# Two blocks' last residual added by VectorE from PSUM, the 14th down chunk on 128 rows, and a new written order

## The chip, the cores and the metric

The kernel runs on one core of a Trainium2 chip. A core has TensorE (PE, matmuls, with a separate row PEld for the loading of the stationary operand), VectorE (DVE), ScalarE (ACT), GpSimd (POOL) and SyncE (SP, which here issues most transfers). Matmuls write PSUM, the other engines work between PSUM and SBUF. The metric is the device time of one launch in microseconds, as the median of three runs.

## The reference

The layer is a convolution block (A) with a gated feed-forward block (B) behind it, both with a residual. There are 2048 tokens of width 640; the hidden width of B is 1728. Inputs are bf16. Cut to what matters:

```python
def _A_ref(q, k, v, shift_k, ssm_k, ssm_D):
    k_shift = sum(k_pad[:, t:t + S, :] * shift_k[:, ks - 1 - t] for t in range(4))
    kv = k_shift * v
    y = irfft(rfft(kv, 2 * S) * rfft(ssm_k, 2 * S))[:S]        # causal convolution, per channel
    return q * (y + kv * ssm_D)

def _B_ref(x, w_gate, w_up, w_down):
    return (silu(x @ w_gate) * (x @ w_up)) @ w_down

x = A_q
h = x + _A_ref(_layernorm(x), A_k, A_v, A_shift_k, A_ssm_k, A_ssm_D)
return h + _B_ref(_layernorm(h), B_w_gate, B_w_up, B_w_down)
```

The hidden width 1728 is 13 chunks of 128 and one of 64. The 64-wide chunk is the "14th chunk" of the title.

## The kernel before, in words

**Blocks.** The tokens are cut into four blocks of 512 (0 to 3). A token tile is the 128 tokens of a block with the same remainder by 4, so a block has four of them, called positions 0 to 3. The convolution is done as block-wise transforms: matmuls against cosine and sine tables (`halves` and `quads`, matmul lines 581 and 619), products of spectra on VectorE (`prod`, line 783), and the inverse transform by matmuls (`inverse`, lines 939 and 944). The short filter over four tokens is done by many small matmuls that use the array in row groups of 32 or 64 rows (`taps`, line 732).

**Work of one block i.** Its x, k and v are loaded (`x2`, `kT2`, `v2` are the loads of block 2, and so on), `tp` and `xf` are the taps and the forward transform, `p` the products, `yb` the butterflies ahead of the inverse, `iv` the inverse. Behind each `iv` tile stands a chain of small steps: `ive` (ScalarE out of PSUM), `ivg` (VectorE, gate with x), `ivm` and `ivs` (ScalarE, mean and square), `ivv` (VectorE), `ivr` (GpSimd, power), `ivn` (normalised row) and `ht` (a transposing DMA into `hnT`). `hnT` is the moving operand of the feed-forward matmuls. `kt`, `kf`, `kb`, `kc` prepare the spectra of the filter in blocks of their own.

**Feed-forward (`ffn`).** Gate and up products are made in two halves of 256 tokens (positions 0, 1 and 2, 3). For each half there are four groups of chunks; `fg` and `fu` are the matmul groups (line 1049, 20 matmuls of 256 columns, 15 in the last group), `sg` is silu on ScalarE into `gu`, `su` a scaled copy of the up part into `ub`, `mu` the product on VectorE. There is one buffer `ub`, so each `su` waits for the `mu` before it. The fourth group holds chunk 12 and the 64-wide chunk 13; its gate and up columns are packed in one stationary tile `PK` (64 gate rows above 64 up rows), so `sv` copies the up part of chunk 13 from PSUM rows 64 to 127.

**Down projection.** `dn` accumulates 14 chunks into two PSUM halves of 320 columns (line 1135; line 1012 for the last token tile, which is split in two). For chunk 13 the rows are shared out: `gd` copies rows 0 to 63 of `gu[:, 13]` to rows 64 to 127 (lines 1111 and 1112), the weight's columns 0 to 319 lie on rows 0 to 63 and its columns 320 to 639 on rows 64 to 127, and the two 64-row matmuls use different row groups of the array (`PAIR`). Odd positions begin with chunk 13 and even ones end with it.

**Last residual.** For blocks 0, 1 and 2 (`RD`), `rs` moves the down result and the mean from PSUM to a buffer `RB` (line 1151 on ScalarE, line 1152 on VectorE), and `ra` adds `RB` onto x by an accumulating DMA from the GpSimd queue (`addto`, line 568). There is one `RB`. For block 3 a VectorE instruction adds PSUM, mean and x in one step (line 1156; line 1018 for the split tile). `out` stores the tile from the SP queue.

**PSUM.** The eight banks are used as four units of two banks. Each matmul group opens one unit (`tp` with 32-row groups opens two) and must wait until the group that had the unit before has been read out.

**Order.** `PLAN` holds, for each engine, the written order of all its steps, and the unit of each PSUM tile. An engine runs its list strictly in that order, with waits where a step depends on another engine. 

Of the kernel before, what the change touches and what calls it, by code (L numbers as in the profile page):

```python
# [50 lines left out]
class _Graph:  # L51
# [131 lines left out]
    def emit(self, block):  # L183
# [84 lines left out]
    "act":  # L268
# [9 lines left out]
    "dve":  # L278
# [15 lines left out]
        "806 ",  # L294
    "units":
        "0113201022031012033321231021332312133313321010001232312221313201230311022320230103301222001112012120120312322323013103"
        "23101021312302023330210213103130021301200122003201320321302",
# [948 lines left out]
```

## Time and profile before

| what | value |
|---|---|
| median of three runs | 254.49 us (254.41 to 254.68) |
| profiled execution, its own time | 254.13 us |
| span of the program in that execution | 252.2 us |
| busy PE / DVE / ACT / POOL | 243.4 / 195.5 / 184.7 / 58.7 us |
| granted TensorE clock | 1.0 |

A row of the timeline has the start and the length in microseconds, the engine, the line, the operation, the tiles written and read, and in brackets the idle time before it with the step that ended it. A row of the chain of waits has a start, a length and what filled it. A matmul's length in the profile contains its latency; matmuls overlap, so the pace of a row of matmuls is its length divided by their count.

### The profile page before, as it was taken

To read this page: it belongs to the slowest core of one execution; us is meant where nothing else is said; L and a number is where in the kernel's file an instruction comes from. 1 tells how busy PE (TensorE), PEld (TensorE's weight loads), DVE (VectorE), ACT (ScalarE), POOL (GpSimd) and SP (SyncE) were. 2 spreads that over 40 slices of the span, in tenths; PEclk is the share of its full clock that TensorE was granted. 3 is DMA by queue.
4 is the path that set the end of the run, shared out by engine and by line. 5 is a ranking of instruction groups with operands and counts; after the bars stand their busy time and mean duration, and the time that the engine had idled before them with its cause. 6 is when DMAs were issued, how large, how long until landed. Compare 5 with 4: busy or idle time off the path is not lost.

```text
span 252.2 us, 5601 instructions
## 1 busy us (share of the span) xinstructions
PE 243.4 (96%) x2405; PEld 190.7 (76%) x2405; DVE 195.5 (78%) x249; ACT 184.7 (73%) x303; POOL 58.7 (23%) x62
## 2 busy tenths in 40 slices
PE   7998997999999999999999999999999999999995
PEld 3776574688887867888888765888886678888763
DVE  2899999999989999999999896989959321312322
ACT  2499999999897994678999699478982856543500
POOL 1000033443113457602103333211141122100000
PEclk9999999999999999999999999999999999999999
DMA  6999999989994465999914718795871144300003
GB/s 212 338 316 222 389 381 292 142 154 169 274 176 78 141 104 109 174 169 216 208 19 76 189 26 82 169 232 99 146 140 26 23 85 79 81 0 3 0 29 104
DMA packets 39063, 37.04 MB, mean 147 GB/s; under 512 B 21235, under 2 KB 34046, under 8 KB 39038
## 3 DMA queue, kind: packets, MB, share of 16 engines
q1 hardware_dynamic: 31648, 23.56, 35.0%
q0 software_dynamic: 7376, 13.11, 30.7%
q8 instruction: 19, 0.31, 0.5%
q14 instruction: 6, 0.05, 0.0%
q10 hardware_dynamic: 14, 0.01, 0.0%
HBM read 16.29 MB, written 2.62 MB: 75 GB/s over the span
## 4 chain that ended last, share of the span: by engine, by line
PE 73%; DVE 11%; DMA 8%; ACT 5%; issue 1%; SPq 0%; DVEq 0%
PE ps L1049 45%; PE ps L1135 18%; PE ps L581 4%; DMA kvo<-in_A_v_dram 3%; DVE C L561 2%; PE ps L944 2%; DVE tt L783 2%; DMA hnT<-qo 2%; PE ps L1012 2%; DMA k0n<-in_A_k_dram 2%; PE ps L732 1%; DVE kvo L755 1%; DVE Y L783 1%; DMA xh<-RB 1%; DVE kvo L748 1%
## 5 line engine op out<-in xcount | busy, mean ns | idle before, releaser
L1135 PE MATMUL ps<-Wd,gu 128*128 128x320 bf16 (+1 forms) x420 | 58.4, 300 | 0.3 <-ACT qo L954 0.3
L1135 PEld LDWEIGHTS ps<-Wd,gu 128*128 128x128 bf16 (+1 forms) x420 | 38.9, 97 | 18.7 <-issue 2.8
L783 DVE TENSOR_TENSOR tt<-XH,C 128x2560 bf16<-128x2560 bf16 (+1 forms) x29 | 45.1, 1576 | 0.2
L1070 DVE TENSOR_TENSOR gu<-gu,ub 128x1024 bf16<-128x1024 bf16 (+1 forms) x32 | 19.9, 621 | 20.9 <-ACT gu L1057 12.9
L1057 ACT ACTIVATE gu<-ps 128x1024 bf16<-128x1024 f32 (+1 forms) x32 | 29.0, 913 | 8.7 <-PE ps L1049 8.5
L1049 PE MATMUL ps<-hnT,GB 128*128 128x256 bf16 x280 | 34.2, 273 | 0.0
L1049 PE MATMUL ps<-hnT,UB 128*128 128x256 bf16 x280 | 33.7, 273 | 0.0
L1062 ACT ACTIVATE ub<-ps 128x1024 bf16<-128x1024 f32 x24 | 24.5, 1020 | 12.4 <-PE ps L1049 9.7
L1049 PEld LDWEIGHTS ps<-hnT,UB 128*128 128x128 bf16 x280 | 27.4, 98 | 3.3
L1049 PEld LDWEIGHTS ps<-hnT,GB 128*128 128x128 bf16 x280 | 27.2, 98 | 3.3
L1049 PE MATMUL ps<-hnT,UA 128*128 128x256 bf16 x240 | 28.8, 273 | 0.0
L1049 PE MATMUL ps<-hnT,GA 128*128 128x256 bf16 x240 | 28.2, 273 | 0.4 <-DMA hnT<-qo 0.4
L1049 PEld LDWEIGHTS ps<-hnT,GA 128*128 128x128 bf16 x240 | 23.4, 98 | 3.5 <-DVE OS L458 0.8
L1049 PEld LDWEIGHTS ps<-hnT,UA 128*128 128x128 bf16 x240 | 23.3, 98 | 3.1 <-ACT XH L455 0.2
L857 POOL TENSOR_TENSOR mv<-mv,half 128x1 f32<-128x1 f32 x16 | 15.7, 982 | 32.9 <-DVE mv L855 28.5
L581 PE MATMUL ps<-KT,tab 128*128 128x320 bf16 x128 | 19.4, 300 | 2.3 <-DVE KT L457 1.1
L860 ACT ACTIVATE qo<-xh 128x640 bf16<-128x640 bf16 x28 | 20.6, 736 | 1.2 <-DMA hnT<-qo 0.5
L954 ACT ACTIVATE qo<-ps,one,st 128x640 bf16<-128x640 f32 x16 | 13.8, 883 | 8.1 <-PE ps L939 7.1
L568 POOL DMA_DIRECT2D xh<-RB x12 | 10.8, 899 | 38.0 <-ACT RB L1151 31.6
L581 PEld LDWEIGHTS ps<-KT,tab 128*128 128x128 bf16 x128 | 11.3, 98 | 8.8 <-DVE KT L457 1.4
L857 POOL TENSOR_TENSOR st<-st,half 128x4 f32<-128x4 f32 x4 | 7.2, 1792 | 38.7 <-DVE st L852 31.4
L862 ACT ACTIVATE qo<-xh,mv 128x640 bf16<-128x640 bf16 x16 | 13.2, 830 | 0.2
(115 smaller groups left out, 377.0 us busy)
## 6 DMA issues: line engine op xcount, KB each, us to landing
C<-US POOLq DMA_DIRECT2D x6, 640.0 KB, 6.6
kc<-in_A_ssm_k_dram SPq DMA_DIRECT2D x4, 640.0 KB, 9.9
xh<-in_A_q_dram SPq DMA_DIRECT2D x4, 640.0 KB, 6.9
out_dram<-xh SPq DMA_DIRECT2D x15, 160.0 KB, 1.9
kvo<-in_A_v_dram SPq DMA_DIRECT2D x3, 640.0 KB, 7.6
xh<-RB POOLq DMA_DIRECT2D x12, 160.0 KB, 2.9
C<-C POOLq DMA_DIRECT2D x2, 640.0 KB, 7.6
Wd<-in_B_w_down_dram SPq DMA_DIRECT2D x1, 1280.0 KB, 11.8
```

Of the source, the lines that this page charges most:

```text
L568: return g.add(name, "pool", lambda e, n: e.dma_start(dst, src, accum_op=ALU.add, max_dma_last_dim=4096), ("acc", 2 * int(np.prod(dst.shap ...
L581: last = e.matmul(pt.f(c, W), tab[:, f, cs, j], src[:, j, c * W:(c + 1) * W], start=(j == js[0]), stop=(j == js[1]))
L783: g.add(nm, "dve", lambda e, n_: e.tensor_tensor(out=d, in0=a, in1=b, op=op), ("sb", n * D), r=[a, b], w=[d])
L857: g.add(name + "r", "pool", lambda e, n: e.tensor_tensor(out=dst, in0=tmp, in1=hf, op=ALU.pow), ("pp", 4), r=[tmp, half[:]], w=[dst])
L860: g.add(name + "m", "act", lambda e, n: e.activation(out=junk, in_=x, func=ACTF.Identity, scale=-1.0 / D, accum_out=sm), ("aa", D, 0), r=[ ...
L862: g.add(name + "s", "act", lambda e, n: e.activation(out=junk, in_=x, func=ACTF.Square, bias=sm, accum_out=sq), ("aa", D, 1), r=[x, sm], w ...
L954: g.add(nm + "e", "act", lambda e, n, pt=pt, q2=q2, s=s, j=j: e.activation(out=q2, in_=pt.f2(W), func=ACTF.Identity, scale=s[:, 3, j:j + 1 ...
L1049: last = e.matmul(pt.f(q // 2, 256, o=256 * (q % 2)), w[:, c, f0:f0 + P], hnT[:, c, cols], start=(c == 0), stop=(c == NC5 - 1))
L1057: g.add("sg%d.%d%d" % (i, h, gp), "act", lambda e, n, pa=pa, gv=gv, nf=nf: e.activation(out=gv, in_=pa.f(0, 256 * nf).rearrange("p (f x) - ...
L1062: g.add("su%d.%d%d" % (i, h, gp), "act", lambda e, n, pb=pb: e.activation(out=ub[:].rearrange("p b x -> p (b x)"), in_=pb.f(0, 1024), func ...
L1070: g.add("mu%d.%d%d" % (i, h, gp), "dve", lambda e, n, gv=gv, ubv=ubv: e.tensor_tensor(out=gv, in0=gv, in1=ubv, op=ALU.mult), ("sb", 256 * ...
L1135: last = e.matmul(pt.f(c, W), gu[k, fb, col(i, j)], Wd[k, fb, c * W:(c + 1) * W], start=st, stop=sp)
```

## The change

`RD` goes from (0, 1, 2) to (0,): in blocks 1 and 2, `rs` becomes the VectorE instruction of line 1156 and the eight `ra` transfers are gone. `PAIR` goes from True to False: chunk 13 of the down projection is two 128-row matmuls like the other chunks, rows 64 to 127 of its weight are set to zero once (`wz`, a memset), both column halves of the weight come by one load, the eight `gd` copies are gone, and `mu` of the fourth group is cut into two products of 256 columns (`mu` on 128 rows, `mv` on 64). Chunk 13 always comes last in `dn`. All five orders and the PSUM units are new.

The orders of the diff hold step numbers; these are counted again in the new kernel, since some steps are gone and some new. By name, these are the moves of steps between engines: `k0e2` ACT to DVE, `kf0e.011` DVE to ACT, `xf0e.110` ACT to DVE, `kte2.1` DVE to ACT, `kf2e.110` and `kf3e.011` ACT to DVE, `ke2.4` ACT to DVE, `la1.3x`, `la3.1x` ACT to DVE, `la2.3x`, `la3.3x` DVE to ACT, `xf3e.10`, `xf3e.20` DVE to ACT, `xf3e.01` ACT to DVE, `lp0`, `lp2`, `la2w` DVE to POOL, `la3w` POOL to DVE. In the SP queue `x1` moves from behind `UA` to just behind `kT1`, `itab` from ahead of `GA` to behind it, `WdC` from ahead of `itab` to behind `ht0.0`, and `WdA` from behind `ht0.2` to ahead of it.

```diff
-    RD = (0,1,2)
+    RD = (0,)
-    PAIR = True
+    PAIR = False
...
+        if not PAIR:
+            g.add("wz", "pool dve", lambda e, n: e.memset(Wd[:, 13, :], 0.0), ("pm", D), w=[Wd[:, 13, :]])
...
+                    if nf == 2 and not PAIR:
+                        for nm, a, b in (("mu", gu[:, 12, cols], u12), ("mv", gu[0:FL, 13, cols], u13)):
+                            g.add("%s%d.%d%d" % (nm, i, h, gp), "dve", lambda e, n, a=a, b=b: e.tensor_tensor(out=a, in0=a, in1=b, op=ALU.mult),
+                                  ("sb", 256), r=[a, b], w=[a])
+                        continue
...
-                if col(i, j).start // P % 2:
+                if PAIR and col(i, j).start // P % 2:
                     seq = [13] + seq[:-1]
...
-                                k = slice(0, P) if fb < 13 else slice(FL * c, FL * c + FL)
+                                k = slice(0, P) if fb < 13 or not PAIR else slice(FL * c, FL * c + FL)
```

By name, the new order of the PE list in the stages that the prediction speaks of:

```
block 1:       dn0.3 fu1.00 tp2.0 tp2.4 fg1.00 fu1.01 xf2.30 xf2.11 xf2.10 xf2.31 fg1.01 xf2.01 xf2.20 fg1.02 ...
into block 2:  dn1.1 iv2.1 iv2.0 dn1.2 xf3.21 iv2.3 xf3.31 xf3.11 iv2.2 xf3.01 xf3.30 dn1.3 xf3.10 xf3.00 fu2.00 xf3.20 fg2.00 ...
into block 3:  dn2.0 dn2.3 iv3.1 iv3.0 dn2.0b iv3.3 iv3.2 dn2.2 dn2.1 fu3.01 ...
```

More of the change, by code (lines that the diff above doesn't have):

```diff
@@ L260 @@
     "pe":
[7 rows of a table removed]
[L268 removed]
[9 rows of a table removed]
[L278 removed]
[9 rows of a table removed]
[7 rows of a table added]
+    "act":
[8 rows of a table added]
+    "dve":
[9 rows of a table added]
     "pool":
[L289 to L290 removed]
+        "19 17 15 16 129 178 169 14 130 162 202 187 196 228 201 230 229 340 285 360 361 398 370 380 371 289 381 293 403 297 390 "
+        "391 408 417 419 521 522 420 523 555 546 564 573 672 580 585 693 698 686 720 711 729 738 ",
     "sp":
[L292 to L294 removed]
+        "0 2 3 8 4 6 9 7 235 10 12 13 300 299 232 301 231 11 233 236 234 238 477 180 171 239 237 189 198 286 478 373 363 290 "
+        "383 294 298 393 476 642 466 643 469 472 557 548 475 641 566 575 722 713 740 634 631 731 637 786 792 640 795 789 798 ",
     "units":
[L296 to L297 removed]
+        "0113201110031233023322032112133122022022013131311010020012031302103102303230323202230310001112101132012200132110312033"
+        "23203003231302131032201033321012223100202011233010331201320",
     "fills": {
@@ L1133, in mm @@
                                     continue
-                                k = slice(0, P) if fb < 13 else slice(FL * c, FL * c + FL)
+                                k = slice(0, P) if fb < 13 or not PAIR else slice(FL * c, FL * c + FL)
                                 last = e.matmul(pt.f(c, W), gu[k, fb, col(i, j)], Wd[k, fb, c * W:(c + 1) * W], start=st, stop=sp)
@@ L1138, in ffn @@
                     fbs = [f for f in part if f != "id"]
-                    mode = (int(part[0] == 13), int(part[-1] == 13))
+                    mode = (int(part[0] == 13), int(part[-1] == 13)) if PAIR else ()
                     g.add("dn%d.%d%s" % (i, pos(i, j), "b" if len(parts) > 1 and part is parts[1] else ""), "pe", mm,
-                          ("mm", W, 2 * len(part) - (13 in part)) + mode,
+                          ("mm", W, 2 * len(part) - (PAIR and 13 in part)) + mode,
                           r=[gu[:, f, col(i, j)] for f in fbs] + [Wd[:, f] for f in fbs] + ([x, ident] if "id" in part else []),
```

6 lines of the change are left out of this document (1 added, 5 removed), and 49 rows, old and new, of the table PLAN.

## The prediction

> **What bounds the kernel now.** I read the page's busy line first, then a table of windows by stage, then the chain of waits and the timelines at the places where TensorE stood still.
>
> ```profile
> PE 243.4 (96%) x2405; PEld 190.7 (76%) x2405; DVE 195.5 (78%) x249; ACT 184.7 (73%) x303; POOL 58.7 (23%) x62
> ```
>
> ```profile
> 12.00:42.50 30.50, 27.43 (x341) 19.11 (x339) 30.27 (x47) 30.05 (x48) 3.99 (x2) 1.00 1.06 324
> 42.50:140.40 97.90, 97.89 (x1050) 79.73 (x1050) 96.48 (x102) 85.61 (x143) 34.17 (x30) 1.00 0.80 150
> 140.40:157.50 17.10, 16.32 (x118) 10.56 (x117) 13.79 (x25) 14.35 (x28) 5.29 (x7) 1.00 0.55 92
> 157.50:204.50 47.00, 47.00 (x399) 38.19 (x400) 37.27 (x51) 30.87 (x52) 11.47 (x12) 1.00 0.59 116
> 204.50:249.50 45.00, 45.00 (x383) 36.52 (x381) 10.91 (x19) 19.59 (x29) 2.85 (x4) 1.00 0.19 47
> ```
>
> The columns are the window and its length, then busy time (and count) of PE, PEld, DVE, ACT, POOL, the clock, the DMA share and GB/s. From 42.5 to its last matmul TensorE is idle only between 140.4 and 157.5; so there the end is set by the sum of matmul slots and by what stalls them. From 12 to 42.5 VectorE (30.27 of 30.5) and ScalarE (30.05) are both full and TensorE waits for them. So the change can act in three ways: fewer TensorE slots, a longer or shorter evacuation stage before 42.5, and stalls made or removed later.
>
> **Part 1: the 14th chunk.** The chain of waits shows each down stage as one piece of matmuls (start, length, count):
>
> ```profile
> 56.43 2.17 PE ps L581 x16
> ...
> 74.98 3.77 PE ps L1135 x28
> 78.76 2.28 PE ps L944 x16
> ...
> 89.76 7.66 PE ps L1135 x56
> ...
> 97.86 3.77 PE ps L1135 x28
> ...
> 187.13 7.55 PE ps L1135 x56
> ...
> 196.31 7.66 PE ps L1135 x56
> ...
> 228.09 2.72 PE ps L1135 x20
> ...
> 236.81 8.61 PE ps L1135 x64
> 245.41 4.13 PE ps L1012 x28
> ```
>
> A plain 320-column matmul paces at 2.17/16 = 0.1357 us, so 28 plain ones are 3.80 us, four tiles 15.20. Paired, chunk 13 should be one slot instead of two (27 slots, 3.66), but the tiles take 3.77 to 3.86: the pair loses about 0.1 us on each entry into and exit from the 64-row mode. The exit is seen behind the tile (2.28 against 2.17 for 16 slots). With these exits block 0 costs 3.77 + 7.66 + 3.77 + 0.11 = 15.31, block 2, with as much for its exits, 15.21 + 0.11 = 15.32, block 3 2.72 + 8.61 + 4.13 = 15.46. Without the mode: savings of 0.11, 0.12 and 0.26. For block 1, whose tiles stand alone between other work, I put 0.16, the mean of these. **Sum -0.65 us**, between -0.3 (only block 0's and 2's rows hold, no more in 1 and 3) and -0.9.
>
> The tap matmuls keep their modes. `tp2.4` loses its place between two paired tiles, where its entry was free; by the 0.1 us per switch above it now pays one: **+0.1** (0 to +0.2).
>
> The Trainium skill ("TensorEngine Tiling (Array Packing)", section "Overview") gives up to 2x for a contract dimension of 64 or less, which speaks against this change. Its section "Key Properties" says that a change of mode drains the array, which is what the 0.1 us steps show; with free switches the change would instead cost 16 slots of 0.136.
>
> **Part 2: VectorE and ScalarE.**
>
> ```profile
> L1156 DVE SCALAR_TENSOR_TENSOR xh<-ps,st,xh 128x640 bf16<-128x640 f32 x3 | 2.7, 884 | 6.4 <-PE ps L1135 6.4
> L1152 DVE TENSOR_SCALAR RB<-ps,st 128x640 bf16<-128x640 f32 x3 | 2.6, 880 | 3.8 <-DMA xh<-RB 3.8
> L1151 ACT ACTIVATE RB<-ps,st 128x640 bf16<-128x640 f32 x9 | 7.1, 790 | 4.6 <-PE ps L1135 3.2 <-DMA xh<-RB 1.2
> L1070 DVE TENSOR_TENSOR gu<-gu,ub 128x512 bf16<-128x512 bf16 x8 | 3.4, 419 | 1.0 <-ACT ub L1068 0.9
> L1112 DVE COPY gu<-gu 64x256 bf16<-64x256 bf16 x5 | 1.1, 221 | 0.2
> ```
>
> VectorE gains 8 x 0.884 = 7.07 us and loses 3 x 0.880 = 2.64 and 5 x 0.22 = 1.1 of `gd`; each cut `mu` costs between 0.22 (the 64-row copy) and 0.42 for each half, taken at 0.28, so 8 x (0.56 - 0.42) = +1.1. Net +4.4 on 195. ScalarE loses 5 x 0.79 and three `gd`. GpSimd loses eight issues, and the memset `wz` stands in its idle time (3.99 busy of the 30.5 us before 42.5). It adds a wait: in SP's queue `WdC` must follow it, and `WdA`, `ht0.2` and `ht0.3` stand behind. None of this is on the path by itself: in blocks 2 and 3 VectorE has 9.7 us free in the window 157.5 to 204.5, and the `rs` only hold PSUM units that are wanted later. If that cover were gone, each `rs` would cost 0.88.
>
> **Part 3: the start.**
>
> ```profile
> 6.30 1.51 ACT L455 ACTIVATE kT<-ps 128x1024 bf16<-128x1024 bf16 x2 [3.48 <-PE ps L528]
> 7.36 1.23 DVE L457 COPY kT<-ps 128x1024 bf16<-128x1024 bf16 x1 [1.78 <-PE ps L528]
> ...
> 8.52 3.08 DVE L755 TENSOR_TENSOR kvo<-ps,v 128x512 bf16<-128x512 f32 x5
> ...
> 11.66 1.53 PE L581 MATMUL ps<-kvo,tab 128*128 128x320 bf16 x10 [0.42 <-DVE kvo L755]
> ```
>
> `k0e2` moves to VectorE, so its two copies follow each other: 6.30 + 2 x 1.23 less the overlap = 8.68. The first `kv` is then held by `tp0.2` and VectorE to 8.72 instead of 8.52, and the five `kv` end 0.2 us later, which shifts `xf0`. **+0.2** (0 to +0.5).
>
> ```profile
> 21.36 3.56 ACT L455 ACTIVATE KT<-ps 128x1280 bf16<-128x1280 bf16 x3
> 24.71 1.40 ACT L455 ACTIVATE KO<-ps 128x640 bf16<-128x640 f32 x2
> 25.88 1.43 ACT L455 ACTIVATE C<-ps 128x640 bf16<-128x640 f32 x2
> ```
>
> From there to 58 I followed both lists by their pitch: from start to start (24.71 - 21.36)/3 = 1.12 us for a `kte`, (25.88 - 24.71)/2 = 0.585 for an evacuation. ScalarE takes `kte2.1` (+1.1) and gives back `kf2e.110` and `kf3e.011`, 0.6 each, later; VectorE does the reverse. On ScalarE the three `kte` start 0.2 late, and by the extra `kte2.1` its first step for the inverse, `iv0.1e`, comes near 37.0 instead of 35.5. VectorE reaches `yb0.0` near 33.2 instead of 32.7, then runs `yb0.1`, `kv1.4`, `kb1`, the gates and `kte3.1` to about 41.0, `kv1.0` to 42.2 and `kf2e.110`, whose unit `xf1.000` needs, to 42.9. Before, TensorE waited at the same spot for `kte3.1` and went on at 42.5. So the wait falls at nearly the same place: `xf1.000` near 43.0 with one group fewer still to do, then 15.3 us of matmuls with small waits to 58.6, against 58.5. Behind it `mu0.00` comes late on VectorE (63.4, before 57.5) and with it `su0.01`, by the one `ub`; the unit of `fu0.01` comes free near 65, and `fg0.11` wants it at 66.8. **0**, with +1.1 if ScalarE's extra step shows in full and -0.5 if half of the stage's smaller waits close. In SP's queue `itab` now waits for `x1`, `UA`, `v1` and `GA` while the DMA engines are full (share 1.06 in this window); `iv0.1` wants it near 35, and I take 0, up to +1. `yb1.0` then ends at about 78.9, just when TensorE wants `iv1.1`: **+0.1**.
>
> **Part 4: block 1's transform.** Before, no more than two `xf2` matmul groups stood together; now four do, each half as long as its evacuation.
>
> `fu1.01` keeps one unit, so `xf2.31` needs the unit of `xf2.30` and `fg1.01` that of `xf2.11`. Evacuations pace at 0.585, a group's two matmuls at 0.27: the fourth group waits 0.3 and `fg1.01` 0.36. Together with `fg1.00`, which waits for `rs0.3` behind `su1.00` (0.15): **+0.8** (0 to +1.5).
>
> **Part 5: into block 2.**
>
> ```profile
> 134.23 2.91 DMA xh<-RB
> ...
> 152.81 4.60 DMA hnT<-qo
> ```
>
> ```profile
> hnT<-qo SPq DMA_TRANSPOSE x16, 3.2
> ```
>
> ```profile
> 145.10 1.23 DVE L748 TENSOR_TENSOR kvo<-XT,kvo 128x2048 bf16<-128x2048 bf16 x1 [0.69 <-DMA kvo<-in_A_v_dram]
> ```
>
> ```profile
> 151.18 3.95 PE L1135 MATMUL ps<-Wd,gu 64*128 64x320 bf16 x28 [0.26 <-ACT qo L954]
> 154.96 2.09 PE L619 MATMUL ps<-kvo,tab 128*128 128x320 bf16 x12
> 157.50 0.71 PE L1049 MATMUL ps<-hnT,GA 128*128 128x256 bf16 x5 [0.45 <-DMA hnT<-qo]
> ```
>
> `v3` stood in the SP queue behind `out1.0`, and that behind the accumulating transfer (2.91 us); VectorE then waited for `v3` with the whole chain to `ht2.0` queued behind it. The last twelve `xf3` matmuls (1.63 at pace) took 154.96 to 157.50, so 0.9 us was lost there and some 0.4 before `dn1.3`: 1.25 in all. Now `rs1.0` ends the wait of `out1.0` on VectorE directly and `v3` comes some 3 us earlier. The tiles between `dn1.1` and the feed-forward are 3 x 3.80 + 4 x 0.543 + 8 x 0.271 = 15.7 us; one `xf3` group stands behind `fu2.00`. VectorE's new list, counted from the start of `dn1.1`: `mu1.12` 1.3 to 2.0, `yb2.4` to 3.4, the cut `mu` to 4.0, `yb2.5` to 5.4, then `iv2.1g`, `kv3`, `iv2.0g` to 8.0 and `rs1.1` to 8.8; `rs1.2` waits for the end of `dn1.2` (3.8 + 1.1 + 3.8, and latency: 9.0) and ends at 9.9; behind it are queued `iv2.1n`, `xf3e.31` and `iv2.0n`, which ends at 11.5. Before, `ht2.0` went out at 152.8 - 140.4 = 12.4. It lands 3.2 to 4.6 us on (the median of all, and the chain's). What is late next is again `ht2.0`, by 0 to 0.65; I take 0.25, and 0.2 for units. **-0.8** (-1.25 to 0).
>
> Blocks 2 and 3 I followed in the same way and found no new stall: counted from the start of `dn2.0`, `yb3.4` ends near 5.5 and `iv3.1`, now a part tile earlier, wants it at 6.5; `rs2.3` frees its unit 0.25 us before `dn2.2`, the tightest place; `ht3.0` lands some 0.9 us ahead of its use.
>
> **Sum:** -0.65 + 0.1 + 0.2 + 0 + 0.1 + 0.8 - 0.8 = -0.25 us on the profiled execution's 254.13 (span 252.2 and 1.9 around it), so 253.9. That execution lies 0.36 below the median of 254.49; on the median's scale the forecast is **254.2**.
>
> **Rivals.**
>
> *The half-1 columns of block 0 come late (slower).* `WdA` now goes out ahead of `ht0.2` and `ht0.3` in SP's queue.
>
> ```profile
> 59.63 1.47 SPq L447 DMA_DIRECT2D Wd<-in_B_w_down_dram x1
> ```
>
> ```profile
> Wd<-in_B_w_down_dram SPq DMA_DIRECT2D x1, 1280.0 KB, 11.8
> ```
>
> `WdA` can go at about 57, when the last `kf3` has read its rows. If it takes 11.8 us as before and the transposes queue behind it, they land near 70, and `fg0.11` wants them at 66.8: +3, so 257.2. It decides when the second lands after 66.8. Against it: the accumulating transfers that shared `WdA`'s time start only near 61 now. Price 257.2, chance 0.13.
>
> *The evacuation stage falls behind (slower).* ScalarE's extra `kte2.1` shows in full (+1.1), with no recovery: 255.3. For it: both engines are full from 12 to 42.5. Against it: VectorE's relief there. Chance 0.2.
>
> *Stalls fall away (faster).* `ht2.0` is on time without the accumulating transfer beside it (-0.45), and the `xf2` groups fit (-0.7): 253.0. For it: the `ht` median of 3.2. Chance 0.22.
>
> *The modes were nearly free.* Then the pair's loss comes back as 16 slots of 0.136 in place of the saving: 254.2 + 0.65 + 2.2 = 257.0. Against it stand the down rows above. Chance 0.03.
>
> *The forecast's own case*, 253.6 to 254.9: chance 0.42.
>
> **Numbers.** What a measurement of this kernel can tell from no change is about 0.2%, 0.5 us: faster is below 254.0, slower above 255.0. Below 254.0 lie the faster rival and some 0.16 of the forecast's case: 0.38. Above 255.0 lie the three slow ones but for some 0.06 of the second: 0.30. Between: 0.32. The range goes from 252.9 to 256.4.
>
> **What would show it.** Down stages of 3.80 us per tile without an exit step; `xf0` at 11.86; `xf1` near 43.0; waits at `xf2.31` and `fg1.01`; `fu2.00` some 15.5 to 16 us behind `dn1.1`; no TensorE idle time in blocks 2 and 3. It would be wrong if `fg0.11` waits for `hnT`, or if TensorE stalls in blocks 2 or 3 behind a late `mu` or `rs`.

## The result, and the profile after

The changed kernel takes **256.33 us** (median of 6, 256.02 to 257.44) against 254.45 for the kernel before beside it: a ratio of 1.008, with a 95% interval of 1.0054 to 1.0105. It is slower by about 0.8%, where 254.2 was forecast: inside the range, but in the other direction. Ratios here leave out executions more than 1.5% above the fastest of the same kernel (among them one of 892.68 us in the run `e15_taps` and one of 649.08 in `e16_taps_xf2`), while the medians count all, so a ratio can lie below the quotient of the medians.

The profiled execution took 257.44, the longest of the six, with a span of 255.2 (before: 254.13 and 252.2). So 0.3 us of the difference lies outside the span, and 3.0 inside.

The page's busy line, and the windows by stage with the columns of the prediction, the stages cut at the same kinds of work as before:

```profile
PE 243.8 (96%) x2405; PEld 193.3 (76%) x2405; DVE 200.0 (78%) x257; ACT 178.1 (70%) x293; POOL 57.1 (22%) x57
```

```profile
12.00:42.50 30.50, 28.07 (x350) 19.51 (x347) 30.06 (x45) 30.50 (x47) 2.89 (x2) 1.00 1.00 306
42.50:140.40 97.90, 94.44 (x1008) 76.35 (x1008) 94.58 (x102) 80.43 (x137) 40.74 (x34) 1.00 0.79 157
140.40:162.80 22.40, 22.40 (x179) 16.83 (x177) 20.73 (x32) 17.85 (x33) 2.20 (x3) 1.00 0.39 66
162.80:252.60 89.80, 89.77 (x764) 74.44 (x761) 47.24 (x73) 47.14 (x77) 10.37 (x11) 1.00 0.33 68
```

From 42.5 to 140.4 TensorE was never idle before; now it is idle for 97.90 - 94.44 = 3.46 us and does 42 matmuls fewer. The stage into block 2 has no idle time any more, and blocks 2 and 3 have 0.03. So the loss lies ahead of 140.4, in the start and in blocks 0 and 1. GpSimd, of which the prediction said only that it loses work, is busy 40.74 us there instead of 34.17.

The places where TensorE stands still, from its timeline after (88.81 is `fu0.12`, 107.65 and 111.07 are `fg1.00`, 113.36 and 114.59 the four `xf2` groups, 115.18 `fg1.01`, 156.23 `dn1.3`, 160.59 `fu2.00`):

```profile
88.81 2.36 PE L1049 MATMUL ps<-hnT,UB 128*128 128x256 bf16 x20 [1.40 <-ACT ub L1062]
...
105.78 1.88 PE L732 MATMUL ps<-diag,kT 32*128 32x128 bf16 x126
107.65 2.25 PE L1049 MATMUL ps<-hnT,GA 128*128 128x256 bf16 x19
111.07 0.27 PE L1049 MATMUL ps<-hnT,GA 128*128 128x256 bf16 x1 [1.17 <-issue]
...
113.36 0.98 PE L619 MATMUL ps<-kvo,tab 128*128 128x320 bf16 x6
114.59 0.45 PE L619 MATMUL ps<-kvo,tab 128*128 128x320 bf16 x2 [0.25 <-ACT OS L453]
115.18 1.27 PE L1049 MATMUL ps<-hnT,GA 128*128 128x256 bf16 x10
...
156.23 3.98 PE L1140 MATMUL ps<-Wd,gu 128*128 128x320 bf16 x28
...
160.59 2.35 PE L1049 MATMUL ps<-hnT,UA 128*128 128x256 bf16 x20
```

The stalls are 1.40 us ahead of `fu0.12`, 1.17 inside `fg1.00` with nothing that the trace shows being waited for (the profile calls it issue), and, in the `xf2` groups, 114.59 - (113.36 + 6 x 0.1357) = 0.42 and 115.18 - (114.59 + 2 x 0.1357) = 0.32.

How much later a step of TensorE starts than before, at six places; the second column is the execution of the run `e7_after_third` (256.37), the one that lies nearest to the median:

| place | profile of 257.44 | profile of 256.37 | what lies in the piece |
|---|---|---|---|
| `xf0` | +0.60 | +0.47 | the start |
| `fu0.01` | +0.82 | +0.69 | the evacuation stage, +0.22 |
| `dn0.1` | +2.40 | +2.23 | the wait at `fu0.12` |
| `dn1.1` | +4.57 | +3.43 | the `xf2` groups 0.73, the stall in `fg1.00` 1.17 and 0.22 |
| `dn2.0` | +3.37 | +2.22 | Part 5, -1.2 |
| last matmul | +3.04 | +1.90 | blocks 2 and 3, -0.3 |

**Where the wait at `fu0.12` comes from.** The timeline of all engines but TensorE around 77 us, first of the kernel before, then after. `st<-st,half` is `la1r`, the power on GpSimd for block 1's first norm; the row above it or two above is `la1v`, which releases it; `OS<-Y` is `yb1.0`.

```profile
75.96 0.16 DVE L855 TENSOR_SCALAR st<-st 128x4 f32<-128x4 f32 x1
76.03 0.42 DVE L1070 TENSOR_TENSOR gu<-gu,ub 128x512 bf16<-128x512 bf16 x1
76.21 1.13 POOL L857 TENSOR_TENSOR st<-st,half 128x4 f32<-128x4 f32 x1 [2.55 <-DVE st L855]
76.48 0.22 DVE L1112 COPY gu<-gu 64x256 bf16<-64x256 bf16 x1
76.73 1.49 DVE L561 TENSOR_TENSOR OS<-Y 128x2560 bf16<-128x2560 bf16 x1
```

```profile
77.30 0.16 DVE L855 TENSOR_SCALAR st<-st 128x4 f32<-128x4 f32 x1
77.38 0.37 DVE L881 TENSOR_SCALAR xh<-xh,st 128x640 bf16<-128x640 bf16 x1
77.55 5.30 POOL L857 TENSOR_TENSOR st<-st,half 128x4 f32<-128x4 f32 x1 [3.98 <-DVE st L855]
77.67 1.48 DVE L561 TENSOR_TENSOR OS<-Y 128x2560 bf16<-128x2560 bf16 x1
79.07 1.48 DVE L783 TENSOR_TENSOR tt<-XH,C 128x2560 bf16<-128x2560 bf16 x1
80.47 1.48 DVE L561 TENSOR_TENSOR Y<-Y 128x2560 bf16<-128x2560 bf16 x1
82.95 1.66 ACT L954 ACTIVATE qo<-ps,one,st 128x640 bf16<-128x640 f32 x2 [2.52 <-POOL st L857]
```

The same power on 4 elements per partition took 1.13 us before and 5.30 now. ScalarE's two `ive` (line 954) scale by its result and wait 2.52 us for it; behind them in ScalarE's list stand the two statistics of each tile and `su0.11`, which empties the PSUM unit that `fu0.12` wants. Before, a short copy (`gd0.0`, line 1112) stood behind `la1v`; it wrote partitions 64 to 127, and it and the step behind it started 0.03 us **after** their predecessors' ends (76.48 against 76.45, 76.73 against 76.70). Now each VectorE step starts 0.08 us **ahead** of its predecessor's end (79.07 against 79.15), up to 81.95, where VectorE stands still; the power ends 82.85, 0.90 later. Before, it ended at 77.34, 0.89 behind 76.45, the first such gap. That is the reading that the experiments test.

### The profile page after: what moved, and what is told of

Read it like the earlier page. It is cut to its first block, busy times and chain, and to the rows that moved or that the text cites. A ratio compares the mean times of both kernels' runs of the same rounds, so it can differ in the third digit from the quotient of the medians.

```text
span 255.2 us, 5587 instructions
## 1 busy us (share of the span) xinstructions
PE 243.8 (96%) x2405; PEld 193.3 (76%) x2405; DVE 200.0 (78%) x257; ACT 178.1 (70%) x293; POOL 57.1 (22%) x57
## 4 chain that ended last, share of the span: by engine, by line
PE 63%; DVE 20%; DMA 6%; ACT 5%; POOL 2%; issue 2%; SPq 1%; ACTq 0%
PE ps L1049 36%; PE ps L1140 21%; DVE tt L783 5%; DVE Y L783 3%; DMA kc<-in_A_ssm_k_dram 3%; DMA hnT<-qo 3%; DVE C L561 3%; POOL st L857 2%; PE ps L939 2%; PE ps L1012 1%; PE ps L619 1%; PE ps L732 1%; DVE bns L847 1%; DVE XH L561 1%; DVE C L681 1%
## 5 line engine op out<-in xcount | busy, mean ns | idle before, releaser
L1140 PE MATMUL ps<-Wd,gu 128*128 128x320 bf16 x420 | 59.0, 299 | 0.0
L1140 PEld LDWEIGHTS ps<-Wd,gu 128*128 128x128 bf16 x420 | 41.0, 98 | 15.7 <-ACT XH L453 0.2
L1075 DVE TENSOR_TENSOR gu<-gu,ub 128x1024 bf16<-128x1024 bf16 x24 | 16.5, 688 | 24.9 <-ACT ub L1062 20.4
L857 POOL TENSOR_TENSOR mv<-mv,half 128x1 f32<-128x1 f32 x16 | 14.0, 873 | 65.6 <-DVE mv L855 61.1
L581 PE MATMUL ps<-KT,tab 128*128 128x320 bf16 x128 | 20.3, 300 | 1.1 <-ACT KT L453 0.8
L857 POOL TENSOR_TENSOR st<-st,half 128x4 f32<-128x4 f32 x4 | 10.0, 2504 | 37.0 <-DVE st L852 23.1
L1161 DVE SCALAR_TENSOR_TENSOR xh<-ps,st,xh 128x640 bf16<-128x640 f32 x11 | 9.7, 879 | 5.6 <-PE ps L1140 5.6
```

The source lines that it names most:

```text
L581: last = e.matmul(pt.f(c, W), tab[:, f, cs, j], src[:, j, c * W:(c + 1) * W], start=(j == js[0]), stop=(j == js[1]))
L857: g.add(name + "r", "pool", lambda e, n: e.tensor_tensor(out=dst, in0=tmp, in1=hf, op=ALU.pow), ("pp", 4), r=[tmp, half[:]], w=[dst])
L1075: g.add("mu%d.%d%d" % (i, h, gp), "dve", lambda e, n, gv=gv, ubv=ubv: e.tensor_tensor(out=gv, in0=gv, in1=ubv, op=ALU.mult), ("sb", 256 * ...
L1140: last = e.matmul(pt.f(c, W), gu[k, fb, col(i, j)], Wd[k, fb, c * W:(c + 1) * W], start=st, stop=sp)
```

## The experiments

The kernel before ran beside each of them (medians 254.21 to 254.57). The theories T1 to T8 in the expectations are numbered as they came up; the ones that decide are named in the text.

| run | kernel | median, range, count | ratio (95%) | `la1r` |
|---|---|---|---|---|
| `e1_after_again` | changed kernel | 259.11 (257.31 to 259.64, 6) | 1.0156 (1.0124 to 1.0189) | 5.30 |
| `e7_after_third` | changed kernel | 256.37 (1) | | 5.30 |
| `e11_after_fourth` | changed kernel | 256.80 (255.91 to 258.95, 6) | 1.0111 (1.0072 to 1.0151) | 5.30 |
| `e2_hold_la1` | changed, VectorE waits for `la1r` | 258.70 (255.95 to 259.12, 6) | 1.0131 (1.0092 to 1.017) | 2.50 |
| `e8_hold_again` | the same | 255.90 (1) | | 2.50 |
| `e3_nopair` | before + `PAIR = False` | 256.47 (255.35 to 258.22, 6) | 1.0081 (1.0051 to 1.011) | 6.01 |
| `e4_rd0` | before + `RD = (0,)` | 256.40 (255.99 to 257.40, 6) | 1.0068 (1.0046 to 1.009) | 1.13 |
| `e5_nopair_hold` | e3, VectorE waits for `la1r` | 255.65 (254.53 to 256.73, 12) | 1.0035 (1.0012 to 1.0058) | 1.03 |
| `e6_la1late` | before, `la1v` behind `gd0.0` | 254.17 (254.01 to 255.66, 12) | 0.999 (0.9971 to 1.001) | 2.20 |
| `e9_la1swap` | changed, `la1.3x` ahead of `la1v` | 256.82 (255.75 to 259.37, 6) | 1.0105 (1.0061 to 1.0149) | 5.01 |
| `e10_nopair_la1` | e3, `la1v` behind `mv0.03` | 256.43 (255.01 to 257.84, 9) | 1.009 (1.0061 to 1.0119) | 5.61 |
| `e12_fgfirst` | e9, taps behind `fg1.00` | 258.63 (258.45 to 258.82, 5) | 1.0166 (1.0136 to 1.0196) | 5.00 |
| `e13_hole` | changed + one short copy | 255.13 (253.85 to 257.86, 12) | 1.0032 (1.0006 to 1.0058) | 1.10 |
| `e14_nopair_hole` | e3 + the same copy | 254.49 (253.75 to 255.19, 12) | 1.0001 (0.9982 to 1.0019) | 1.19 |
| `e15_taps` | e13, the taps apart | 255.44 (254.49 to 892.68, 12) | 1.0045 (1.0014 to 1.0077) | |
| `e16_taps_xf2` | e15, `xf2` two and two | 257.13 (254.29 to 649.08, 12) | 1.0047 (1.0016 to 1.0078) | 1.10 |
| `e17_hole2` | e13 + a second copy | 255.32 (254.78 to 255.85, 12) | 1.0029 (1.0009 to 1.0049) | 1.10 |
| `e18_hole2_xf2` | e17, `xf2` two and two | 254.97 (254.05 to 255.52, 12) | 1.0011 (0.9989 to 1.0034) | 1.10 |

**The change again, and its two halves by themselves.** The changed kernel unedited; the changed kernel with a wait; and each of the two switches alone in the kernel before, on its old orders:

```diff
  e2  p02.d on VectorE waits for la1r
  e3  before.py:  -PAIR = True       +PAIR = False      (gd gone, mu cut in two, wz added; old orders)
  e4  before.py:  -RD = (0,1,2)      +RD = (0,)         (ra gone, rs of blocks 1 and 2 on VectorE; old orders)
```

> The changed kernel once more, unedited, to see what recurs. Theory T1 (a stall that the new orders make in every execution: GpSimd's la1r takes 5.3 us instead of 1.1 while VectorE issues back to back, and iv1.1, su0.11 and fu0.12 come about 1.75 us late): la1r again 4 to 6 us, fu0.12 again about 1.2 us after its unit was wanted, median 256.2 to 256.5. Rival T3 (accidents of the one profiled execution): la1r 1 to 2 us, no issue stall of 1.2 us inside fg1.00 and kc0 landing before 10.2 us; if only the last two fall away, the profiled time comes to some 256.0 with la1r still long.

> The changed kernel with one wait more: VectorE's p02.d, its third step behind la1v, waits for GpSimd's la1r, so VectorE stands still while the small step runs. T1: la1r ends within 1.5 us of its start, iv1.1e goes out near 80, su0.11 and fu0.12 are on time, minus 1.2 to 1.7 us, so 254.6 to 255.1. Rival T2 (la1r is late for another reason, such as its input, or the lost time lies in other parts of the orders): the time stays within 0.3 of the changed kernel, or VectorE's idle time of about 0.5 us shows as up to 0.8 us slower.

> The kernel before, its own orders and transfers, with Part 1 alone: the 14th chunk of the down projection on 128 rows, with the zeroed rows and the second product in two pieces. The prediction's step: minus 0.65 (0.3 to 0.9), so 253.5 to 254.2 beside 254.45. The rival that the 64-row modes were nearly free: 16 slots of 0.136 more, plus 2.2, 256.6. A third way: the saving is real in TensorE's slots but the kernel's end does not follow, because it goes into the waits ahead of block 2 (dn3's ends earlier by 0.3 alone).

> The kernel before, its own orders, with the last residual of blocks 1 and 2 alone moved to VectorE from PSUM. The prediction's Part 5: v3 and ht2.0 come earlier, minus 0.8 (0 to 1.25), so 253.2 to 254.4 beside 254.45. A rival: VectorE is full between block 1's down projection and block 2, and the rs of 0.88 us queued ahead of the chain to ht2.0 eat the gain: within 0.3 of the kernel before, or up to 1 us slower.

The changed kernel, measured again unedited, gave 259.11 (256.2 to 256.5 was expected), 256.37 and 256.80. It is always slower than before, by 0.7 to 1.6%, and its executions spread more than those of the kernel before beside it (2.3 us against 1.5 in e1, 3.0 against 2.2 in e11). The wait of e2 brought `la1r` to 2.50 and the stall at `fu0.12` to 0.47, and its profiled execution is 255.95 against 257.31 for that of e1; but five of its six executions were longer (up to 259.12), and they were not profiled. As a whole e2 settled nothing; e8 with the same kernel gave 255.90, with 0.70 at `fu0.12`.

Each half alone is slower than the kernel before, e3 by 0.8% and e4 by 0.7%, and for different reasons. In e3 the power is held up as in the changed kernel, with no copy behind `mu`:

```profile
76.32 0.48 DVE L1070 TENSOR_TENSOR gu<-gu,ub 128x256 bf16<-128x256 bf16 x2
...
76.50 6.00 POOL L855 TENSOR_TENSOR st<-st,half 128x4 f32<-128x4 f32 x1 [2.79 <-DVE st L853]
...
82.60 1.66 ACT L952 ACTIVATE qo<-ps,one,st 128x640 bf16<-128x640 f32 x2 [2.69 <-POOL st L855]
```

In e4, `gd0.0` is still there and the power takes 1.13. Of the 2.3 us by which its last matmul is later than before, 0.3 lie in the start, 0.8 in blocks 2 and 3, and 1.0 in the stage that Part 5 is about. VectorE's and TensorE's timelines of e4 there:

```profile
145.45 0.22 DVE L1109 COPY gu<-gu 64x256 bf16<-64x256 bf16 x1
145.70 0.88 DVE L1153 SCALAR_TENSOR_TENSOR xh<-ps,st,xh 128x640 bf16<-128x640 f32 x1
146.50 1.22 DVE L745 TENSOR_TENSOR kvo<-XT,kvo 128x2048 bf16<-128x2048 bf16 x1
```

```profile
152.56 3.95 PE L1132 MATMUL ps<-Wd,gu 64*128 64x320 bf16 x28 [0.52 <-ACT qo L951]
...
157.49 0.45 PE L616 MATMUL ps<-kvo,tab 128*128 128x320 bf16 x2 [0.17 <-DVE xh L1153]
158.22 0.72 PE L616 MATMUL ps<-kvo,tab 128*128 128x320 bf16 x4 [0.28 <-DVE OS L455]
```

`v3` landed at 140.30 instead of 145.08, as Part 5 says, and VectorE waits for it no longer. But the 0.88 us of `rs1.0` take the place of the 0.69 us of waiting, and with the `rs` in the old order the transposing transfer `ht2.0` goes out 13.37 us behind `dn1.1` instead of 12.44. So the gain of Part 5 is there only with the new orders, and the `rs` is not hidden without them.

**What holds the power up.** From the kernel before and from e3, three edits of `la1v`'s neighbours; and one of the changed kernel:

```diff
  e5  e3, mu0.03 on VectorE waits for la1r
  e6  before:  la1v mu0.03 gd0.0 yb1.0   ->  mu0.03 gd0.0 la1v yb1.0
  e9  after:   la1v la1.3x yb1.0         ->  la1.3x la1v yb1.0
  e10 e3:      la1v mu0.03 mv0.03 yb1.0  ->  mu0.03 mv0.03 la1v yb1.0
```

> The kernel before with Part 1 alone, as in the run before it, and one wait: VectorE's mu0.03, the first step behind la1v, waits for GpSimd's la1r. In the run without the wait la1r took 6.01 us (before: 1.13) and ended 0.90 us after VectorE first stood still; fg0.12 came 1.57 late. Theory T4 (the step gd0.0 that Part 1 removes was the only place where VectorE let go between la1v and iv1.0g, and la1r ran in that hole): with the wait la1r ends within 1 us, no stall at fu0.12, minus 1.3 to 1.6 us against the run without it, so 254.0 to 255.2 by the medians, and 253.5 to 253.9 if nothing else of Part 1 costs time. Rival: the stall belongs to the cut products mu and mv on ScalarE's side, and the wait changes nothing or adds its 0.7 us.

> The kernel before with one step moved by two places: VectorE's la1v goes out behind gd0.0 instead of ahead of mu0.03, so that no step with another start partition stands between la1v and iv1.0g. T4: la1r takes 4.5 to 5.5 us instead of 1.13, ends 0.90 us after VectorE's first pause near 81.6, and fg0.12 or fu0.12 stalls by 1.2 to 1.6: 255.6 to 256.2 beside 254.5. Rival (the cause is the product's two halves or the removed transfers, not the hole): la1r stays near 1.1 us and the time within 0.4 of before, since la1v itself comes only 0.6 us later.

> The changed kernel once more, for a profile of one of its other executions: they differ by up to 3 us. If instruction or load accidents make the difference, other steps than la1r and fu0.12 show it: stalls put down to issue behind the tap matmuls (fg1.00: 0.9 to 1.2 so far), or kc0 landing later than 10.2 us. If la1r itself makes it, it takes 6 to 8 us here.

> The changed kernel with VectorE's wait for la1r once more, for a second profile. With la1r fixed at about 2.5 us, a time near 256 again means that T1 holds and the longer executions have another cause; a time near 259 shows that cause's place in TensorE's steps.

> The changed kernel with two neighbours of VectorE's list exchanged: la1.3x (0.37 us) ahead of la1v instead of behind it, so that yb1.0 (1.48 us) runs when GpSimd's la1r arrives. No wait is added. Theory T5 (GpSimd gets in at the end of the VectorE step that runs when its own step arrives, if the next VectorE step starts later than some 0.2 us after that; otherwise it is locked out until VectorE stands still): la1r 2.2 us instead of 5.3, no stall at fu0.12, minus 1.2 to 1.6 us against the unedited changed kernel beside it. Rival (only a pause of VectorE lets GpSimd in): la1r again about 5.3 us, the same time within 0.3.

> The kernel before with Part 1 alone, and la1v behind mv0.03, right ahead of yb1.0. T5: la1r 2.2 us instead of 6.01, no stall of 1.57 behind fg0.12, so what is left is Part 1's own gain, which the traces so far put at 0.5 in the down tiles less 0.3 at tp2.4: 254.0 to 254.5 beside 254.5. Rival (la1r locked out as without the move): 256 to 256.5. A third way: 255 to 255.7, if Part 1 has another cost that the profiles have not shown.

> The changed kernel unedited, timed beside its two edited forms on the same chip: 256.0 to 256.6 as in most looks, or 257.3 to 259.6 as in the rounds of the second look; la1r 5.3 us in either.

With the wait in e3's orders (e5) the power takes 1.03, VectorE stands idle 1.16 us for it, and the ratio falls from 1.0081 to 1.0035. The expectation for e6 (T4: no gap behind `la1v` any more, so `la1r` in 4.5 to 5.5 and 255.6 to 256.2) failed, and so did T5, that the neighbouring step decides (e9, e10: 5.01 and 5.61, no faster). The timeline of e6:

```profile
76.38 0.22 DVE L1109 COPY gu<-gu 64x256 bf16<-64x256 bf16 x1
76.63 0.17 DVE L852 TENSOR_SCALAR st<-st 128x4 f32<-128x4 f32 x1
76.71 1.49 DVE L558 TENSOR_TENSOR OS<-Y 128x2560 bf16<-128x2560 bf16 x1
76.89 2.20 POOL L854 TENSOR_TENSOR st<-st,half 128x4 f32<-128x4 f32 x1 [3.32 <-DVE st L852]
78.11 1.48 DVE L780 TENSOR_TENSOR tt<-XH,C 128x2560 bf16<-128x2560 bf16 x1
```

Here the power ended at 79.09, 0.89 behind the end of `yb1.0` (78.20), though the next step had started at 78.11 without a gap. So GpSimd got in where there was a gap, but a gap isn't needed. The next power of block 1, `iv1.1r`, shows the same: in the kernel before it ran from 89.41 to 91.10, and it ended 0.42 behind the end of a VectorE step (90.68) whose successor had started at 90.59; in the changed kernel it ended 0.41 behind such a step. Why GpSimd got in at these places and in e9 and e10 not, stays open.

**A gap put in.** T7: what helped was not the time that `gd0.0` took but that it writes from another start partition on, which makes the gaps. So a copy of 64 x 16 elements, whose result nothing uses, goes in from partition 0 to partition 64, in the changed kernel and in e3:

```diff
+    if (i, h) == (0, 0):
+        g.add("hole", "dve", lambda e, n: e.tensor_copy(out=hole[FL:P, :], in_=gu[0:FL, 13, 0:16]), ...)
  e13 after: la1v la1.3x yb1.0         ->  la1v la1.3x hole yb1.0
  e14 e3:    la1v mu0.03 mv0.03 yb1.0  ->  la1v mu0.03 mv0.03 hole yb1.0
```

> The changed kernel with one small VectorE step more, put where gd0.0 stood before: behind la1.3x a copy of 64 x 16 elements from partition 0 into partition 64 of a scratch tile (no result uses it). Theory T7 (VectorE lets GpSimd in where a step starts on another partition than the one ahead of it, since it then begins only when that one has ended; gd0.0 was such a step): la1r 0.9 to 2.4 us instead of 5.0 to 5.3, no stall of 1.57 at fu0.12, minus 1.2 to 1.6 us: 254.6 to 255.2 where the changed kernel has 256.3, or that much under its 256.8 of the last look. Rival (gd0.0 mattered through its length or its place in the queue, not through its partitions): la1r again 5 us, same time.

> The kernel before with Part 1 alone and the same small copy behind mv0.03, where gd0.0 stood. T7: la1r 1.1 to 2.3 us instead of 6.0, fu0.12 on time, 254.0 to 254.6: Part 1's own gain of some 0.2 to 0.4. Rival: la1r 5 to 6 us and 256 to 256.5. Third: la1r is short and the time is still above 255, so that Part 1 costs something in the start that the profiles have not named.

The timeline of e13:

```profile
76.68 0.37 DVE L879 TENSOR_SCALAR xh<-xh,st 128x640 bf16<-128x640 bf16 x1
76.85 1.10 POOL L855 TENSOR_TENSOR st<-st,half 128x4 f32<-128x4 f32 x1 [4.03 <-DVE st L853]
77.08 0.17 DVE L1073 COPY hole<-gu 64x16 bf16<-64x16 bf16 x1
77.27 1.49 DVE L559 TENSOR_TENSOR OS<-Y 128x2560 bf16<-128x2560 bf16 x1
...
86.50 2.35 PE L1047 MATMUL ps<-hnT,UB 128*128 128x256 bf16 x20
```

The last row is `fu0.12`, which now waits for nothing; nor does it in e14. The copy and the step behind it start 0.03 and 0.02 behind their predecessors' ends, and the power takes 1.10 and ends at 77.95, 0.90 behind the first gap. Nothing else of the order is changed, VectorE even has a step more, and the changed kernel's median falls by 1.2 us against the first measurement (256.33) and by 1.7 against e11. In e3 it falls by 2.0, to 254.49: with the hold-up gone, dropping the pairing costs and gains nothing that can be measured (1.0001, 0.9982 to 1.0019). This is the experiment that decides: the loss of both kernels in block 0 comes by way of `la1r`, from the want of a step like `gd0.0` behind `la1v`. In e3 `mv0.03`, which writes from partition 0 on, stands in `gd0.0`'s place; in the changed kernel the new order has also put `mu0.03` ahead of `la1v`. That it is the gap that lets GpSimd in is argued, from the 0.90 us behind it: no run has the same copy without a gap, and the copy also differs from most of its neighbours in having one input only.

The Trainium skill ("SBUF — State Buffer", section "Who interferes with whom") says that a VectorE instruction with two SBUF inputs contends with a GpSimd instruction that reads SBUF, that the lock on the shared ports is exclusive, and that the order of issue decides which of the two blocks. The trace agrees that they contend (5.30 against 1.13 and 1.10), but here GpSimd stays out not over one VectorE step but over three and more on end. The Trainium skill ("VectorE: DVE Perf Modes", section "Two Vector instructions with no wait between them") holds an instruction whose start quadrant differs from that of the access before it until all earlier ones have finished; the trace agrees (0.03 us behind the end instead of 0.08 ahead).

**The second power.** e13 still ranges from 253.85 to 257.86. The changed kernel's profile in e11 (258.47) shows what can make one execution long. VectorE's and GpSimd's timeline of e7, and of e11; `mv<-mv,half` is `iv1.0r`:

```profile
88.03 1.48 DVE L783 TENSOR_TENSOR Y<-Y 128x2560 bf16<-128x2560 bf16 x1
88.08 1.87 POOL L857 TENSOR_TENSOR mv<-mv,half 128x1 f32<-128x1 f32 x1 [4.53 <-DVE st L893]
```

```profile
87.47 1.48 DVE L783 TENSOR_TENSOR Y<-Y 128x2560 bf16<-128x2560 bf16 x1
87.52 6.28 POOL L857 TENSOR_TENSOR mv<-mv,half 128x1 f32<-128x1 f32 x1 [4.53 <-DVE st L893]
```

The same code, the same 0.05 us behind the same VectorE step, and once 1.87 us, once 6.28. Of the eleven profiles with this order nine have 1.86 or 1.87 and two 6.28 (the expectation of e17 below counts eleven and two; it also counts three executions of e13 above 256.5, which are two). Before, with `p02.c` ahead of `iv1.1v`, this power took 1.80. T8: a second such copy behind `iv1.1v` takes this chance away, and with it the spread. The edit, and those on the two other losses of block 1, which follow below; e15, e16 and e18 also have other PSUM units, and e16 and e18 the evacuations and a few VectorE steps in an order to fit:

```diff
  e12 after: tp2.0 tp2.4 fg1.00 -> fg1.00 tp2.0 tp2.4;  rs0.3 ahead of su1.00, sg1.00 ahead of ke2.0b;  la1.3x ahead of la1v, as in e9
  e15 e13:   tp2.0 ahead of fu1.00, tp2.4 behind fg1.00;  rs0.3 ahead of su1.00;  p03.c ahead of ke2.4
  e16 e15:   xf2.30 xf2.11 | fg1.01 | xf2.31 xf2.10, two groups and two
  e17 e13:   iv1.1v p02.c -> iv1.1v hole2 p02.c
  e18 e17:   xf2.30 xf2.11 | fg1.01 | xf2.31 xf2.10
```

> The changed kernel with TensorE's fg1.00 ahead of the taps tp2.0 and tp2.4 instead of behind them (and rs0.3 ahead of su1.00 on ScalarE, which frees its unit); la1v is left as it is. Theory T6 (the taps' 252 short instructions use up the loaded instructions before the next block of 16 KB has landed, so TensorE stands still for 0.4 to 1.3 us in fg1.00 or fu1.01; the more ordinary matmuls stand between the block's request and the taps, the smaller it is): from tp2.0's or fg1.00's start, whichever is first, to xf2.30 some 6.3 to 6.6 us instead of 6.4 to 7.6, no stall put down to issue, minus 0.4 to 1.0 us. Rival (the stall is a wait for data or a PSUM unit that the profile doesn't name): it stays, or xf2.30 then waits for kv2.0 by as much and the time is within 0.3.

> As e13, and on TensorE tp2.0 goes out ahead of fu1.00 and fg1.00, tp2.4 behind them (rs0.3 ahead of su1.00 on ScalarE, p03.c ahead of ke2.4 on VectorE, fu1.01 on the PSUM unit of ke2.0b). Theory T6 as the last runs left it (TensorE's instructions come in blocks of 256; instruction 2241 ran 1.4 us after its block had landed in all five profiles with a stall put down to issue, at fg1.00 or fu1.01 alike; taps side by side use up a block in 2 us): now 5.4 us of work lie between instructions 1985 and 2241, so instruction 2241 runs at least 2 us after its block, no stall put down to issue, and fu1.01 waits 0.6 us for ke2.0b instead: minus 0.2 to 0.9 against e13, and a smaller spread of its times. Rival: the spread and the time stay as they are, because the long executions have another cause.

> As e15, and block 1's eight xf2 groups go out two and two between fu1.01, fg1.01, fg1.02, fu1.02 and fg1.03 as they did before the change, with PSUM units and ScalarE's order to fit. Part 4 of the prediction (four groups in a row cost 0.66 at xf2.31 and fg1.01; the profiles showed 0.73 to 0.86): minus 0.5 to 0.9 against e15. Rival: VectorE's xb2 steps or the units make up for it, within 0.3 of e15.

> As e13, and a second small copy of the same kind on VectorE behind iv1.1v, ahead of p02.c. In all profiles of the changed kernel and its kin GpSimd's iv1.0r arrives 0.05 us after p02.c began; it took 1.87 us in eleven of them and 6.27 in two, and those two are executions of 258.5 and 258.6 us. Theory T8 (the long executions are this second lockout, a race that the new order of iv1.1v and p02.c makes close; with a step on another partition in between GpSimd is always first): iv1.0r 1.0 to 2.0 us in the profile, no execution above 256.5 (e13 had three of twelve there), median 254.2 to 255.0. Rival (the spread comes from the first loads and the instruction blocks): the same spread of 4 us as e13, and its median of 255.1.

> As e17, and block 1's xf2 groups two and two as before the change (e16's order, on e13's taps). Part 4 of the prediction: minus 0.4 to 0.8 against e17, no wait of 0.86 at fg1.01, so 253.6 to 254.5 and the first version below the kernel before. Rival: within 0.3 of e17, because xf2.11 then waits for kv2.0 or the stall for instructions at 2241 grows by what is saved.

The timeline of e17:

```profile
86.26 0.14 DVE L854 TENSOR_SCALAR mv<-mv 128x1 f32<-128x1 f32 x1
86.36 0.57 POOL L856 TENSOR_TENSOR mv<-mv,half 128x1 f32<-128x1 f32 x1 [4.78 <-DVE st L892]
86.44 0.17 DVE L1076 COPY hole<-gu 64x16 bf16<-64x16 bf16 x1
86.63 1.49 DVE L782 TENSOR_TENSOR Y<-Y 128x2560 bf16<-128x2560 bf16 x1
```

`iv1.0r` takes 0.57, and twelve executions lie within 1.1 us instead of 4.0. T8 was right on the spread and wrong on the median, which it put at 254.2 to 255.0 and which is 255.32; so most executions of e13 can't have had the long power, if it costs what it seems to. That it is this power that made the long executions of the changed kernel is likely and not shown: it rests on two profiles (e11 and e16, 258.47 and 258.62, both with 6.28) and on the narrow ranges of e17 and e18.

**Block 1.** e12 puts the taps behind `fg1.00`. TensorE's timeline there:

```profile
106.16 2.36 PE L1046 MATMUL ps<-hnT,GA 128*128 128x256 bf16 x20 [0.77 <-ACT RB L1153]
...
111.63 1.26 PE L1046 MATMUL ps<-hnT,UA 128*128 128x256 bf16 x10 [1.29 <-DVE XT L452]
```

The stall inside `fg1.00` is gone, but 0.77 and 1.29 us of other waits stand in its place: `rs0.3` waits for the one `RB`, and `fu1.01` for the unit that VectorE empties late (`ke2.4`). So e12 was no clean test. e15 gained nothing against e13, and its profiled execution, the one of 892.68 us, says nothing on the stall. e16's ratio is no better than e15's, and its profile has the long power. e18 is the clean one: against e17 `xf2` two and two is worth -0.35 us by the medians (expected -0.4 to -0.8; the two ranges overlap), and `fg1.01` waits no more:

```profile
111.50 0.72 PE L618 MATMUL ps<-kvo,tab 128*128 128x320 bf16 x4 [0.36 <-DVE kvo L747]
112.06 1.25 PE L1048 MATMUL ps<-hnT,GA 128*128 128x256 bf16 x10
```

The wait of 0.36 for VectorE ahead of the groups isn't new; in e17 it is 0.34. With both copies and the old arrangement of `xf2`, e18 stands at 1.0011 (0.9989 to 1.0034): it can't be told from the kernel before, and no version was faster than that one. Losses are left in it: its profile takes 51.82 us from `dn0.1` to `dn1.1`, 1.14 more than before, and from there to `dn2.0` 45.46, 1.14 less.

**The stall inside `fg1.00`** (T6), argued and not shown. It stood at 1.17, 0.90, 0.22, 0.59 and 0.82 us in the profiles of the change, e1, e7, e8 and e13, each time ahead of the same matmul, the twentieth of `fg1.00`, and in those of e2, e9, e11, e12, e16, e17, e18 and the kernel before not at all. The page counts a queue of instructions, in the same line before and after:

```profile
q8 instruction: 19, 0.31, 0.5%
```

That is 0.31 MB in 19 pieces, 16 KB each. In the change, a piece landed from 108.6 to 109.5 and the stalled matmul ran at 111.07 (in e1 by 109.2 and at 110.67, in e7 by 108.5 and at 109.94); before, a piece came at 104.0 to 105.0, 2.2 us ahead of the matmuls there. Just ahead of it the 126 small matmuls of `tp2.0` and `tp2.4`, now side by side, use up their instructions in 1.88 us. A supply that falls behind such a burst would look like this. More speaks for the supply: from 42.5 us on the profiles but e15's put nine stalls of TensorE down to issue, these five and four shorter ones at other matmuls (0.43 at `fg1.02` in e5, 0.18 and 0.40 at `fu1.12` in e2 and e16, 0.29 at `fu2.00` in e12), and each ends 1.2 to 1.5 us behind the landing of a piece. But e17 has the same order without the stall, and no run took the cause away alone.

## Why the prediction was wrong, point by point

**The step that failed most is Part 2**: VectorE "loses 3 x 0.880 = 2.64 and 5 x 0.22 = 1.1 of `gd`", counted as a gain, and "none of this is on the path by itself". The sum of busy time was right (+4.4 put, 200.0 - 195.5 = 4.5 measured), the path was not: `gd0.0` was no load on it but the step at which GpSimd's power for block 1 got in. Without it the power takes 5.30 instead of 1.13 us, ScalarE stands 2.52, TensorE 1.40, and `dn0.1` is 1.5 us later than the evacuation stage explains. e13 and e14 show it: a copy of 0.17 us gives back 1.2 to 1.7 and 2.0. The rows that should have warned were there, unquoted: the power at 1.13 with `gd0.0` beside it, and 1.80 for `iv1.0r`, more time for less work. A price that differs so much between rows of one operation depends on its neighbours, and the neighbours were what changed.

**The new order of `iv1.1v` and `p02.c`**, which the prediction did not mention, makes `iv1.0r` take 1.87 or 6.28. By the two profiles with 6.28 it widens the spread upward rather than moving every execution.

**Part 4 was right**, and its two waits were well sized: the fourth group waits 0.42 and `fg1.01` 0.32, where 0.3 and 0.36 were put. Taking the four groups apart gave back less, 0.35 (e18). The stall inside `fg1.00`, 0.2 to 1.2, comes on top and had no term: the taps that now stand side by side ahead of it were priced at a mode switch of 0.1 us alone.

**Part 5 was right and larger**: -1.20 from `dn1.1` to `dn2.0` instead of -0.8, with some 0.1 of Part 1 in it. `out1.0` landed at 138.14 (before 143.57) and `v3` at 140.86; `ht2.0` was issued 11.43 us behind the start of `dn1.1` (put at 11.5), `fu2.00` stands 160.59 - 144.94 = 15.65 behind it (15.5 to 16), and TensorE has no idle time there. Both allowances, 0.25 and 0.2, were not needed. e4 adds that the two switches do not bring this alone.

**Part 1 was mis-sized.** The tiles do run at their pace, with no step behind them, in the chain of waits:

```profile
145.10 3.80 PE ps L1140 x28
...
200.28 7.61 PE ps L1140 x56
```

But between e3 and e6, whose orders agree but for `la1v`, the slots give -0.16, -0.14, -0.02 and -0.22 in blocks 0 to 3 (put at 0.11, 0.16, 0.12, 0.26) and +0.29 around `tp2.4` and `dn0.3` (put at +0.1): -0.25 in all instead of -0.55. Block 2's exit, which the prediction took over from block 0 without a row, isn't there. The rival of free modes (257.0) is out: +2.2 us would show.

**Part 3**: the delay that it priced at the start isn't seen. On VectorE the two copies start at 5.86 and end at 8.22 (put at 8.68), and the first `kv`, at 9.12, waits 0.90 for `v0`, which landed at 9.02 (before: 8.16). How late `xf0` starts differs between executions of one kernel: by +0.60, +0.61, +0.47 and -0.21 in the four profiles of the changed kernel, and by +0.31 in e4, whose start is that of the kernel before. So the 0.2 is neither borne out nor refuted. The evacuation stage costs 0.22 instead of 0, within its bounds; the rival that it falls behind by 1.1 (255.3) came with a fifth of its price. The rival of the late half-1 columns is false: `ht0.3` landed at 65.9 and `fg0.11` did not wait.

**Outside the span** lies some 0.35 us that no step had: time less span is 1.9 before (1.92 in the mean of 11 executions) and 2.3 after (2.30, of 6); e3 alone has 1.95 and e4 2.05. It comes with the new orders (2.2 to 2.4 in the mean of each run that has them, 1.9 to 2.05 of each that has the old ones); its cause is open.

Taken together: the gains that were forecast came (-1.2 and -0.3), the losses that were forecast came too (0.73 and 0.22, and at the start up to 0.6), and a loss of 1.2 to 2 us came through an engine that the prediction had read only by its busy share.

## What to carry to other kernels

Before you remove a short step, look at what runs beside it on the other engines, and compare the rows of one operation with each other: an operation that takes 1.13 and 5.30 us in one shape, or 0.57, 1.87 and 6.28 in another, is waiting for something that has no semaphore. A list of long VectorE steps without a gap can hold up a GpSimd step that a whole chain waits for; here one tiny step that writes from another start partition on let it in. And a part that gains only with a new order should be priced in that order, with what the order does elsewhere counted against it.

## What the runs showed of the hardware

GpSimd's power for block 1 on 128 x 4 elements took 1.0 to 1.2 us where VectorE left a gap or waited at once, 2.2 to 2.5 where it got in behind one long step, and 5.0 to 6.0 where it didn't get in until VectorE stood still; in the profiles of the kernel before, the change, e6 and e13 it ended 0.89 to 0.90 us behind the end of the step at which it got in. The same power on 128 x 1 elements, arriving 0.05 us behind a VectorE step's start, took 1.86 to 1.87 us in nine profiles and 6.28 in two: what decides where there is no gap is open. A VectorE step that writes from another start partition on, and the step behind it, began 0.02 to 0.03 us behind the end of the one ahead instead of 0.08 ahead of it. And TensorE stood still for 0.2 to 1.2 us in nine profiles with no semaphore to be seen, until 1.2 to 1.5 us behind the landing of a 16 KB piece of its instructions; in five of them at the same matmul, behind 126 small ones.
